# One-core FNet + gated MLP in blocks: loads, differences and copies moved to other places in the queues

## The chip, the cores and the metric

The kernel runs on one core of a Trainium2 chip. The metric is the device time of one execution in microseconds, the median of several. Lower is better. The profile is of one execution of its own. Engines are named as the profile names them: PE is TensorE's matmuls and PEld its weight loads, DVE is VectorE, ACT is ScalarE, POOL is GpSimd, SP is SyncE, which issues most of the DMAs.

## The reference

```python
def _A_ref(x, dft_seq_re, dft_seq_im, dft_hid_re, dft_hid_im):
    a = jnp.einsum("bsd,ed->bse", x, dft_hid_re)
    b = jnp.einsum("bsd,ed->bse", x, dft_hid_im)
    y = jnp.einsum("ts,bse->bte", dft_seq_re, a) - jnp.einsum("ts,bse->bte", dft_seq_im, b)
    return y

def _B_ref(x, W_gate, W_up, W_down):
    gate = jnp.einsum("bsd,df->bsf", x, W_gate)
    up = jnp.einsum("bsd,df->bsf", x, W_up)
    gate = gate * (gate > 0)
    h = gate * up
    return jnp.einsum("bsf,fd->bsd", h, W_down)

xn = _layernorm(x, axis=-1)
return x + _A_ref(xn, ...) + _B_ref(xn, W_gate, W_up, W_down)
```

There are 2048 tokens of width 640, the inner width of the gated part is 1728, and everything is float32.

## The kernel before

**Precision.** Every float32 operand is split into a high part and a low part: ScalarE copies it (line 125), which rounds it to the matmul's format, and VectorE subtracts that copy from the original to get the low part (line 126). A product is then three matmuls: high by high (line 131), high by low (line 132), low by high (line 133). So a block of 128 x 1024 costs one ScalarE and one VectorE instruction before TensorE can use it. TensorE needs the high part for the first of the three matmuls and the low part for the second.

**Three stages.** The first stage normalises the tokens in groups of 256 (`next_group`, groups 0 to 7) and multiplies them by the sequence DFT matrices. The second is the gate and up products. The third, opened at line 1089, multiplies the results of both by the hidden DFT matrices and by the down weights, adds the residual and writes the output. All three use a two-by-two block scheme with seven products in place of eight (Winograd's form), so operands are often sums or differences of blocks.

**The last stage.** `project(q)` runs for two halves of the tokens, called pairs here: first q = 1, then q = 0. Each pair has seven products in the order B11, T1, B21, T2, B22, T3, T4, so B22 is the fifth and T4 the seventh. Each product runs over seven units, numbered 0 to 6: units 0 to 2 come from the DFT half (two with 1024 columns, one with 512), 3 to 5 from the gated half, 6 is the rest (64 rows, `short`, in B21, B22 and T4). T4 runs unit 6 before unit 5. A unit's name such as T2.6 means unit 6 of T2. A unit of 1024 columns has 18 matmuls in the products that have three outputs (B11, T1, B21, B22) and 12 in the others.

For each unit there are three steps. `load` issues its DMAs: the raw block of the moving operand (`get`, tile `rw`, or `re` for unit 6) and its weights. The weights are either raw and split on the chip (tile `wr`, then `wt`), in B11, T1, B21 and B22, or already split in DRAM (`wt<-wparts`, line 1148), in T2, T3 and T4. `prepare` forms the difference of raw blocks where the product's name begins with T (line 1162), then splits the block into tile `cb` and the weights into `wt`. `run` issues the matmuls. `drive(4, 2)` calls `load` four units ahead of `run` and `prepare` two units ahead.

Raw blocks stay in 24 buffers (`raws`), since several products use them. With r11, r12, r21, r22 for the four raw blocks of a unit, the differences are made in place: T1 makes r12 := r12 - r11, T2 makes r12 := r22 - r12, T3 makes r11 := r12 - r11 and T4 makes r21 := r21 - r12.

**What sets the order.** SP's and GpSimd's instructions keep the order in which the program issues them. SP waits in that order: a load whose buffer is not free holds back all loads behind it. There are 4 buffers for `wr`, 5 for `wt` and 3 for `cb` (the ring). VectorE's, ScalarE's and TensorE's instructions are put in order by a scheduler when the kernel is built, and each engine works through its queue in that fixed order. `in_turn` (BACK = 3) keeps the steps of `prepare` from running far ahead.

**The result of a product** is read from PSUM by VectorE (`add_y`, line 1222) and, when complete, stored by GpSimd's DMA. T2 adds to the banks that B11 filled, T3 and T4 to the same banks again, so T4's first matmul follows the read of T3's sums.

**Group 4.** In the first stage half of the groups is one block row of the scheme. Before group 4, the sums of groups 0 to 3 are copied from PSUM by ScalarE (`keep_first`, tile `sa`, line 122), and group 4's matmuls (line 499) go on adding to the same banks. `next_group(4)` forms the normalised tokens: VectorE centres them, ScalarE writes their high part to `xs_late` (line 232), VectorE the low part (line 236). In this kernel ScalarE has the high part of the first half of the tokens, then the three copies, then the high part of the second half.

Of the kernel before, what the change touches and what calls it, by code (L numbers as in the profile page):

```python
# [7 lines left out]
F32 = mybir.dt.float32  # L8
# [4 lines left out]
P = 128  # L13
S, D, F = 2048, 640, 1728
KD = D // P
CH = 512
# [3 lines left out]
SG = 2  # L20
NG = S // (P * SG)
NH = NG // 2
# [5 lines left out]
NF = F // P  # L28
REST = F - NF * P
# [29 lines left out]
def fnet_reglu_kernel(  # L59
# [178 lines left out]

    def keep_a21(g, src=None):

        nc.gpsimd.dma_start(xn_block(g, K2, 0).bitcast(F32), ln_place(g)[:, :, K2] if src is None else src)

    def pin(steps):
        return [tc.keep_in_program_order(i) for i in steps]
# [6 lines left out]
    def next_group(g, b, raw, before):  # L251

        xs, bs, mv = ln_tiles(g)
        js = slice(0, SG)
        cs = K14 if g < NH else slice(0, D)
        low = lambda engine, j: pin([engine.tensor_tensor(flat(b, 1)[:, j], raw[:, j], flat(b, 0)[:, j].bitcast(F32), op=OP.subtract)])
        pin(ln_stats(g, xs, bs, mv, js))
        pin([nc.scalar.activation(flat(b, 0), raw, AF.Copy)])
        if before is not None:
            behind_vector(before)  # L260
            for j in range(SG):
                low(nc.gpsimd, slice(j * CH, (j + 1) * CH))
# [11 lines left out]
        if before is None:  # L274
            for j in range(SG):
                low(nc.vector, slice(j * CH, (j + 1) * CH))
        pin(ln_refine(g, mv, js))
        late["ln"] = pin(ln_low(g, xs, j, cs) for j in range(SG)[: 1 if g == NH else SG])[-1].ins
        if g == NH:

            def second():
                late["high"] = pin([ln_high(g, xs, mv, 1, cs)])[0].ins
                late["ln"] = pin([ln_low(g, xs, 1, cs)])[0].ins

            late["second"] = second
        if g < NH:
            late["a21"] = g, xs, mv
# [263 lines left out]
    def first_stream(c, name, g):  # L551
# [537 lines left out]
    for n, b, side in (("wraw", 4, "left"), ("ring2", 3, "left"), ("wts", 5, "left"), ("raws", 24, "left"), ("ends", 4, "right"), ("y", 1, "right")):  # L1089
        open_pools[n] = ctx.enter_context(tc.tile_pool(name=n, bufs=b, side=side, reuse_waits="tile"))  # L1090

    def project(q):
        c0, c1 = 2 * q, 2 * q + 1
        units = [("hid", u) for u in HID_UNITS] + [("f", u) for u in F_UNITS] + [("end", (NF // 2,))]
        raws, B, y = {}, {}, {}
        a, b2 = slice(0, REST), slice(REST, 2 * REST)

        def get(kind, u):
            what, ks = units[u]
            o = raws[kind, u] = (pool("ends").tile([P, 1, CH], F32, name="re") if what == "end" else  # L1100
                                 pool("raws").tile([P, 2, CH], F32, name="rw")[:, : len(ks)])
            col, row = int(kind in ("B12", "B22")), int(kind in ("B21", "B22"))
            if what == "hid":
                nc.sync.dma_start(o, pqd[(c0, c1)[col]][row][:, ks[0] : ks[-1] + 1])
            elif what == "end" and row:
                if col:
                    nc.gpsimd.memset(o[b2], 0.0)
                nc.sync.dma_start(o[a, 0], hrest[q][:, col * CH : (col + 1) * CH])
            else:
                nc.sync.dma_start(o, hd[q][2 * ks[0] + row : 2 * ks[-1] + row + 1 : 2][:, :, col * CH : (col + 1) * CH].rearrange("f p t -> p f t"))  # L1110

        def unit(name, u, first, last):
            what, ks = units[u]
# [5 lines left out]
            def load():  # L1119
                kind = {"T1": "B12"}.get(name, name)  # L1120
                if name == "B11" and (q, u) == (1, 0):
                    return
                if kind in ("B11", "B12", "B21"):
                    get(kind, u)

                ahead = {("B21", 1): 0, ("B21", 3): 1, ("B21", 5): 2, ("T2", 0): 3, ("T2", 2): 4, ("T2", 3): 5, ("T2", 4): 6}.get((name, u))
                if ahead is not None:
                    get("B22", ahead)
                if name == "B11" and ("B11", 0) not in raws:
                    get("B11", 0)  # L1130
                own, sums = [i.rearrange("k p n -> p k n") for i in pair(k0, n)], wparts[:, k0 : k0 + n]
                if short and name == "T4":
                    w = pool("wts").tile([P, 2, 2, 3 * P], F32R, name="wt").rearrange("p k v n -> p (k v n)")[:, : 4 * P]
                    t["w"] = w.rearrange("p (k v n) -> p k v n", k=1, v=2)
                    nc.sync.dma_start(w.bitcast(F32), wend)
                    return
                if short:
                    t["r"] = r = pool("wraw").tile([P, 2, 3 * P], F32, name="wr")[:, :n]
                    if name == "B21":
                        nc.sync.dma_start(r[a], own[1][:, :, : 3 * P])  # L1140
                    else:
                        nc.sync.dma_start(r[a, :, :P], own[1][:, :, 2 * P : 3 * P])
                        nc.sync.dma_start(r[a, :, P:], sums[a, :, Z4 : Z4 + 2 * P])
                    return
                if name in PARTS:
                    w = pool("wts").tile([P, 2, 2, 3 * P], F32R, name="wt").rearrange("p k v n -> p (k v n)")[:, : n * 4 * P]
                    t["w"] = w.rearrange("p (k v n) -> p k v n", k=n, v=2)
                    nc.sync.dma_start(w.rearrange("p (k n) -> p k n", k=n).bitcast(F32), sums[:, :, HIGH + PARTS[name] :][:, :, : 4 * P])  # L1148
                    return
                t["r"] = r = pool("wraw").tile([P, 2, 3 * P], F32, name="wr")[:, :n]  # L1150
                if name in ("B11", "B21"):
                    nc.sync.dma_start(r, own[name == "B21"][:, :, : 3 * P])
                else:
                    z = (Z1, Z4)[name == "B22"]
                    nc.sync.dma_start(r[:, :, :P], own[name == "B22"][:, :, 2 * P : 3 * P])  # L1155
                    nc.sync.dma_start(r[:, :, P:], sums[:, :, z : z + 2 * P])

            def prepare():
# [1 line left out]
                    t.update(lead)  # L1160
                    return
                sub = lambda o, i0, i1: nc.vector.tensor_tensor(o, i0, i1, op=OP.subtract)
                r = lambda kind: raws[kind, u]
# [142 lines left out]
```

## Time and profile before

| | |
|---|---|
| median of three runs | 1029.99 us (1029.58 to 1030.07) |
| the profiled execution | 1030.06 us |
| its span, first to last instruction | 1028.3 us |
| granted TensorE clock | 0.999 |
| TensorE busy | 1021.8 us of 4520 matmuls |
| VectorE busy | 819.2 us |
| ScalarE busy | 434.2 us |
| moved by DMA | 246.02 MB, mean 239 GB/s |

The first stage ends and the second begins near 400 us; the last stage begins near 731 us with q = 1, and q = 0 begins near 877 us. A row of a timeline holds the start, the duration, the engine, the line, the operation, the tiles written and read, the shape, and how often it came; in brackets stands how long the engine was idle before it and what ended that. A row of the windows view holds a stretch, its length and, for PE, PEld, DVE, ACT and POOL, the busy time and the number of instructions; then the granted clock, the share of the DMA engines' time and GB/s. A row of DMA issues holds the tiles, how many, KB each, and the median time from issue to landing. A matmul's end is modelled, so matmuls are compared by their starts: in steady work they stand 0.23 us apart.

### The profile page before, as it was taken

To read this page: it belongs to the slowest core of one execution; us is meant where nothing else is said; L and a number is where in the kernel's file an instruction comes from. 1 tells how busy PE (TensorE), PEld (TensorE's weight loads), DVE (VectorE), ACT (ScalarE), POOL (GpSimd) and SP (SyncE) were. 2 spreads that over 40 slices of the span, in tenths; PEclk is the share of its full clock that TensorE was granted. 3 is DMA by queue.
4 is the path that set the end of the run, shared out by engine and by line. 5 is a ranking of instruction groups with operands and counts; after the bars stand their busy time and mean duration, and the time that the engine had idled before them with its cause. 6 is when DMAs were issued, how large, how long until landed. Compare 5 with 4: busy or idle time off the path is not lost.

```text
span 1028.3 us, 12571 instructions
## 1 busy us (share of the span) xinstructions
PE 1021.8 (99%) x4520; PEld 843.5 (82%) x4520; DVE 819.2 (80%) x1117; ACT 434.2 (42%) x552; POOL 124.3 (12%) x195
## 2 busy tenths in 40 slices
PE   9999999999999999999999999999999999999998
PEld 8888888888888888888888888888888888888886
DVE  7967987998989586788878988887686778866785
ACT  5554453343433333433335443443454433544532
POOL 3431001022110002411110000011000000000000
PEclk9999999999999999999999999999999999999999
DMA  8887734967969885763474665674895838993654
GB/s 304 313 293 287 264 119 170 335 227 255 353 224 339 312 321 163 250 215 133 148 242 153 219 236 215 225 264 148 305 335 171 274 98 272 384 336 119 211 176 160
DMA packets 95326, 246.02 MB, mean 239 GB/s; under 512 B 11488, under 2 KB 35552, under 8 KB 92576
## 3 DMA queue, kind: packets, MB, share of 16 engines
q1 hardware_dynamic: 77088, 173.12, 49.0%
q0 software_dynamic: 18176, 72.10, 18.9%
q8 instruction: 35, 0.57, 0.2%
q14 instruction: 27, 0.22, 0.1%
HBM read 184.09 MB, written 60.05 MB: 237 GB/s over the span
## 4 chain that ended last, share of the span: by engine, by line
PE 97%; DMA 1%; DVE 0%; SPq 0%; ACT 0%; issue 0%; ACTq 0%
PE ps L132 31%; PE ps L131 31%; PE ps L133 31%; PE ps L499 3%; PE ps L528 1%; DMA wr<-in_hid 1%; PE ps L1206 1%; DMA wr<-wparts 1%; PE ps L113 1%; DVE cb L126 0%; ACT cb L125 0%; SPq L1155 0%; DVE wt L126 0%; ACT wt L125 0%; SPq L1148 0%
## 5 line engine op out<-in xcount | busy, mean ns | idle before, releaser
L132 PE MATMUL ps<-cb,wt 128*128 128x512 f32 x410 | 159.9, 390 | 0.6 <-DVE cb L126 0.6
L131 PE MATMUL ps<-cb,wt 128*128 128x512 f32 x410 | 159.7, 389 | 0.3 <-issue 0.3
L133 PE MATMUL ps<-cb,wt 128*128 128x512 f32 x410 | 159.2, 389 | 0.0
L125 ACT ACTIVATE cb<-rw 128x1024 fp32r<-128x1024 f32 x83 | 82.0, 989 | 122.8 <-PE ps L133 105.9
L126 DVE TENSOR_TENSOR cb<-rw,cb 128x1024 fp32r<-128x1024 f32 x83 | 93.1, 1132 | 43.4 <-ACT cb L125 43.3
L125 ACT ACTIVATE cb<-raw 128x1024 fp32r<-128x1024 f32 x71 | 75.4, 1062 | 113.7 <-PE ps L133 106.2
L126 DVE TENSOR_TENSOR cb<-raw,cb 128x1024 fp32r<-128x1024 f32 x71 | 86.8, 1223 | 39.0 <-ACT cb L125 38.7
L131 PE MATMUL ps<-xs_early,gw 128*128 128x512 f32 x260 | 101.2, 389 | 0.0
L133 PE MATMUL ps<-xs_early,gw 128*128 128x512 f32 x260 | 101.2, 389 | 0.0
L132 PE MATMUL ps<-xs_early,gw 128*128 128x512 f32 x260 | 101.1, 389 | 0.0
L132 PEld LDWEIGHTS ps<-cb,wt 128*128 128x128 f32 x410 | 77.0, 188 | 17.6 <-DVE cb L126 1.9
L131 PEld LDWEIGHTS ps<-cb,wt 128*128 128x128 f32 x410 | 77.0, 188 | 17.1 <-ACT cb L125 1.1
L131 PE MATMUL ps<-cb,xs_late 128*128 128x512 f32 x232 | 90.2, 389 | 0.0
L132 PE MATMUL ps<-cb,xs_late 128*128 128x512 f32 x232 | 90.2, 389 | 0.0
L133 PE MATMUL ps<-cb,xs_late 128*128 128x512 f32 x232 | 90.2, 389 | 0.0
L133 PEld LDWEIGHTS ps<-cb,wt 128*128 128x128 f32 x410 | 77.0, 188 | 15.9
L122 ACT ACTIVATE gw<-z 128x1024 fp32r<-128x1024 f32 (+1 forms) x52 | 57.6, 1110 | 76.5 <-DVE z L834 76.5
L131 PE MATMUL ps<-cb,xs_early 128*128 128x512 f32 x226 | 87.9, 389 | 0.0
L132 PE MATMUL ps<-cb,xs_early 128*128 128x512 f32 x226 | 87.9, 389 | 0.0
L133 PE MATMUL ps<-cb,xs_early 128*128 128x512 f32 x226 | 87.9, 389 | 0.0
L122 ACT ACTIVATE u<-ps 128x512 f32<-128x512 f32 x52 | 31.2, 599 | 90.4 <-PE ps L133 90.4
L844 DVE TENSOR_TENSOR gw<-z,gw 128x1024 fp32r<-128x1024 f32 (+1 forms) x52 | 64.7, 1284 | 3.8 <-ACT gw L122 3.8
(183 smaller groups left out, 1972.7 us busy)
## 6 DMA issues: line engine op xcount, KB each, us to landing
raw<-in_dft SPq DMA_DIRECT2D x94, 512.0 KB, 5.8
z<-in_wgu SPq DMA_DIRECT2D x26, 640.0 KB, 3.9
wt<-wparts SPq DMA_DIRECT2D x30, 512.0 KB, 4.4
hd<-ob POOLq DMA_DIRECT2D x26, 512.0 KB, 3.3
wparts<-pw POOLq DMA_DIRECT2D x12, 1024.0 KB, 4.1
rw<-hd SPq DMA_DIRECT2D x24, 512.0 KB, 5.9
tk<-in_dft SPq DMA_DIRECT2D x16, 512.0 KB, 7.3
set<-r POOLq DMA_DIRECT2D x16, 512.0 KB, 3.7
```

Of the source, the lines that this page charges most:

```text
L113: nc.tensor.matmul(ps[:, :P], warm, warm, start=True, stop=True)
L122: return nc.scalar.activation(o, i, AF.Copy)
L125: nc.scalar.activation(hi, src, AF.Copy)
L126: return nc.vector.tensor_tensor(lo, src, hi.bitcast(F32), op=OP.subtract)
L131: nc.tensor.matmul(ps, wh, mh, start=first, stop=False, skip_group_check=more)
L132: nc.tensor.matmul(ps, wh, ml, start=False, stop=False, skip_group_check=more)
L133: nc.tensor.matmul(ps, wl, mh, start=False, stop=last, skip_group_check=more)
L499: start["pe"] = pin([nc.tensor.matmul(E[0, key], xn_part(n * SG + j, d)[v == 1], b[:, int(v == 2), j], start=False, stop=n % NH == NH - 1 ...
L528: pin([nc.tensor.matmul(E[c, key], xn_part(j, d)[v == 1], b[c][0][:, int(v == 2), j], start=j == 0 and v == 0, stop=False)])
L844: tt(self.w[:, 1, cs], self.z[:, cs], self.w[:, 0, cs].bitcast(F32), op=OP.subtract)
L1206: nc.tensor.matmul(B[out], w[:, 0, v, oo : oo + P], b[:, 0, 0], start=False, stop=last and v == 1, skip_group_check=more)
```

## The change

Four edits.

1. In `next_group`, for group 4 everything from the centring of the tokens on (`finish`) runs after the three copies of `keep_first`; before, only the second half's high and low parts did.
2. B22's raw blocks are issued with T1.3, T1.5, B21.0, B21.1, B21.3, B21.4 and B21.5. Before, they were issued with B21.1, B21.3, B21.5, T2.0, T2.2, T2.3 and T2.4.
3. T4's differences are formed in B22's `prepare`, after the split of the B22 block of the same unit, and T4's `prepare` only splits.
4. The first three raw blocks of B11 of the second pair (q = 0) are issued in T4 of the first pair, with its units 1, 3 and 5. For this `raws` is shared by both pairs.

```diff
@@ next_group
-            keep_a21(late.pop("keep"))
+            pin([keep_a21(late.pop("keep"))])
         root, inverse = ln_first(g, mv, js)
         pin([root])
         pin([ln_mean(g, mv, js)])
-        pin([ln_center(xs, mv, 0, cs)])
-        pin([inverse()])
-        pin([ln_high(g, xs, mv, 0, cs)])
-        pin([ln_center(xs, mv, 1, cs)])
-        if g != NH:
+
+        def finish():
+            pin([ln_center(xs, mv, 0, cs)])
+            pin([inverse()])
+            pin([ln_high(g, xs, mv, 0, cs)])
+            pin([ln_center(xs, mv, 1, cs)])
             late["high"] = pin([ln_high(g, xs, mv, 1, cs)])[0].ins
...
+            pin(ln_refine(g, mv, js))
+            late["ln"] = pin(ln_low(g, xs, j, cs) for j in range(SG))[-1].ins
+            if g < NH:
+                late["a21"] = g, xs, mv
+
         if g == NH:
...
+            late["finish"] = finish
+            return
+        finish()
@@ keep_first
             for i, key in enumerate((("e1", 0), ("e1", 1), "v1")):
                 pin([copy(t["first"][:, i], E[c, key])])
-            late["second"]()
+            late["finish"]()
@@ project, load
-                if kind in ("B11", "B12", "B21"):
-                    get(kind, u)
-
-                ahead = {("B21", 1): 0, ("B21", 3): 1, ("B21", 5): 2, ("T2", 0): 3, ("T2", 2): 4, ("T2", 3): 5, ("T2", 4): 6}.get((name, u))
+                if kind in ("B11", "B12", "B21") and (q, kind, u) not in raws:
+                    get(q, kind, u)
+
+                ahead = {("T1", 3): 0, ("T1", 5): 1, ("B21", 0): 2, ("B21", 1): 3, ("B21", 3): 4, ("B21", 4): 5, ("B21", 5): 6}.get((name, u))
                 if ahead is not None:
-                    get("B22", ahead)
+                    get(q, "B22", ahead)
...
+                if name == "T4" and q == 1 and u in (1, 3, 5):
+                    get(0, "B11", u // 2)
@@ project, prepare
                     elif name == "T4":
 
-                        src, at = r("B21"), a if short else slice(0, P)
-                        sub(src[at], src[at], r("B12")[at])
+                        src = r("B21")
...
+                    if name == "B22":
+                        at = a if short else slice(0, P)
+                        sub(r("B21")[at], r("B21")[at], r("B12")[at])
```

In the built program TensorE's order is the same. On SP, B22's and B11's loads stand where the edits put them. On GpSimd the memset that B22.6 needs goes ahead of the stores of the products. On VectorE and ScalarE the scheduler's order changes around the places named, and in T1 and B21 of the first pair and B11 of the second as well.

More of the change, by code (lines that the diff above doesn't have):

```diff
@@ L267, in next_group @@
         pin([ln_mean(g, mv, js)])
-        pin([ln_center(xs, mv, 0, cs)])
-        pin([inverse()])
-        pin([ln_high(g, xs, mv, 0, cs)])
-        pin([ln_center(xs, mv, 1, cs)])
-        if g != NH:
-            late["high"] = pin([ln_high(g, xs, mv, 1, cs)])[0].ins
[L274 to L278, printed above, removed]
-        if g == NH:
[L281 to L287, printed above, removed]
+        def finish():
[3 more added lines that the diff above has]
+            pin([ln_center(xs, mv, 1, cs)])
+            late["high"] = pin([ln_high(g, xs, mv, 1, cs)])[0].ins
+            if before is None:
+                for j in range(SG):
+                    low(nc.vector, slice(j * CH, (j + 1) * CH))
+            pin(ln_refine(g, mv, js))
+            late["ln"] = pin(ln_low(g, xs, j, cs) for j in range(SG))[-1].ins
+            if g < NH:
+                late["a21"] = g, xs, mv
+        if g == NH:
+            late["finish"] = finish
+            return
+        finish()
         if g == NG - 1:
@@ L1090, in fnet_reglu_kernel, with get @@
         open_pools[n] = ctx.enter_context(tc.tile_pool(name=n, bufs=b, side=side, reuse_waits="tile"))
+    units = [("hid", u) for u in HID_UNITS] + [("f", u) for u in F_UNITS] + [("end", (NF // 2,))]
+    a, b2 = slice(0, REST), slice(REST, 2 * REST)
+    raws = {}
+    def get(q, kind, u):
+        what, ks = units[u]
+        o = raws[q, kind, u] = (pool("ends").tile([P, 1, CH], F32, name="re") if what == "end" else
+                                pool("raws").tile([P, 2, CH], F32, name="rw")[:, : len(ks)])
+        col, row = int(kind in ("B12", "B22")), int(kind in ("B21", "B22"))
+        cs = slice(col * CH, (col + 1) * CH)
+        if what == "hid":
+            nc.sync.dma_start(o, pqd[2 * q + col][row][:, ks[0] : ks[-1] + 1])
+        elif what == "end" and row:
+            if col:
+                nc.gpsimd.memset(o[b2], 0.0)
+            nc.sync.dma_start(o[a, 0], hrest[q][:, cs])
+        else:
+            nc.sync.dma_start(o, hd[q][2 * ks[0] + row : 2 * ks[-1] + row + 1 : 2][:, :, cs].rearrange("f p t -> p f t"))
     def project(q):
         c0, c1 = 2 * q, 2 * q + 1
[L1094 to L1110, printed above, removed]
+        B, y = {}, {}
         def unit(name, u, first, last):
@@ L1122, in load @@
                     return
[L1123 to L1126 removed]
+                if kind in ("B11", "B12", "B21") and (q, kind, u) not in raws:
+                    get(q, kind, u)
+                ahead = {("T1", 3): 0, ("T1", 5): 1, ("B21", 0): 2, ("B21", 1): 3, ("B21", 3): 4, ("B21", 4): 5, ("B21", 5): 6}.get((name, u))
                 if ahead is not None:
[L1128 to L1130 removed]
+                    get(q, "B22", ahead)
+                if name == "B11" and (q, "B11", 0) not in raws:
+                    get(q, "B11", 0)
+                if name == "T4" and q == 1 and u in (1, 3, 5):
+                    get(0, "B11", u // 2)
                 own, sums = [i.rearrange("k p n -> p k n") for i in pair(k0, n)], wparts[:, k0 : k0 + n]
@@ L1162, in prepare @@
                 sub = lambda o, i0, i1: nc.vector.tensor_tensor(o, i0, i1, op=OP.subtract)
-                r = lambda kind: raws[kind, u]
+                r = lambda kind: raws[q, kind, u]
                 with in_turn():
```

2 lines of the change are left out of this document (1 added, 1 removed).

## The prediction

> **What bounds the kernel now.** I read the page's first two parts, then TensorE's own timeline wherever one matmul starts later than the usual 0.23 us after the one before, then what the other engines did there. The page first:
>
> ```profile
> span 1028.3 us, 12571 instructions
> PE 1021.8 (99%) x4520; PEld 843.5 (82%) x4520; DVE 819.2 (80%) x1117; ACT 434.2 (42%) x552; POOL 124.3 (12%) x195
> ```
>
> TensorE is busy 99% of the span, and the diff adds or removes no matmul. The change can only fill or open gaps between matmuls. The gaps in the places it touches are these (chain of waits in the first stage; TensorE's timeline at the heads of B22 of the first pair, T4 of the first pair, B11 of the second pair and B22 of the second pair):
>
> ```profile
> by line: PE ps L499 51.8%; PE ps L132 16.5%; PE ps L133 16.4%; PE ps L131 15.9%
> 31.28 4.08 PE ps L499 x18
> 39.44 4.86 PE ps L499 x18
> ```
>
> ```profile
> 820.25 0.39 PE L131 MATMUL ps<-cb,wt 128*128 128x512 f32 x1
> 820.61 0.50 PE L132 MATMUL ps<-cb,wt 128*128 128x512 f32 x1
> ...
> 859.73 0.39 PE L133 MATMUL ps<-cb,wt 128*128 128x512 f32 x1
> ...
> 860.96 0.47 PE L131 MATMUL ps<-cb,wt 128*128 128x512 f32 x1 [0.16 <-issue]
> ...
> 876.93 0.39 PE L131 MATMUL ps<-cb,wt 128*128 128x512 f32 x1
> 877.68 0.50 PE L132 MATMUL ps<-cb,wt 128*128 128x512 f32 x1 [0.36 <-DVE cb L126]
> 878.02 0.39 PE L133 MATMUL ps<-cb,wt 128*128 128x512 f32 x1
> ...
> 966.67 0.39 PE L131 MATMUL ps<-cb,wt 128*128 128x512 f32 x1
> 967.31 0.50 PE L132 MATMUL ps<-cb,wt 128*128 128x512 f32 x1 [0.25 <-DVE cb L126]
> ```
>
> Start to start, less 0.23: group 4 loses 4.86 - 4.08 = 0.78 us, B22 of the first pair 0.13, T4 0.32 (860.96 - 859.73, four starts), the change of pair 0.52, B22 of the second pair 0.41. After such a wait the third matmul is late too (878.02 - 877.68 - 0.23 = 0.11), so four of these places hold 0.11 more each. All that could be won is near 2.6 us, and 0.2% of the run, about what a measurement of this kernel tells from no change, is 2.06 us.
>
> **Group 4's copies first.** ScalarE's timeline there:
>
> ```profile
> 37.85 0.83 ACT L232 ACTIVATE xs_late<-r,mv 128x640 fp32r<-128x640 f32 x1 [1.74 <-DVE mv L211]
> 38.70 1.57 ACT L122 ACTIVATE sa<-ps 128x512 f32<-128x512 f32 x3
> ```
>
> The three copies (1.57 us) empty the sums that group 4's first matmuls add to, and stand behind a scaling that waited 1.74 us for VectorE. What they read was finished at 31.28 + 4.08 = 35.4, so in the new order they go into that idle time, from 36.1 to 37.7, and the scaling still starts at 37.85 and ends at 38.7, before the matmul at 39.4. Gain 0.78; lower bound 0, should another operand be late. In the built order GpSimd's store of a kept block (L241) also goes behind two subtractions, and two first-stage loads change places in SP's queue. The by-line row has only TensorE in this window, so TensorE waits for neither: 0.
>
> **B22's seven blocks earlier, both pairs.** Per pair seven issues on SP move: two go from B21 into T1, one moves up within B21, four go from T2 into B21. The last one needs a memset on GpSimd first. That memset moves ahead of the result stores in GpSimd's queue; it needs nothing but its tile, and GpSimd is busy 12% of the run, so it delays no store. In T1 the traffic is heavy, but what ScalarE waits for there is TensorE freeing the ring, not a load. The stage's row (its last two numbers are the DMA engines' busy share and GB/s) and one such wait:
>
> ```profile
> 755.60:780.10 24.50, 24.50 (x109) 20.29 (x109) 18.82 (x23) 11.83 (x15) 0.00 (x0) 1.00 0.94 334
> ```
>
> ```profile
> 759.98 1.06 ACT L125 ACTIVATE cb<-rw 128x1024 fp32r<-128x1024 f32 x1 [2.71 <-PE ps L133]
> ```
>
> Two blocks more in T1 are 1.05 MB, 3.1 us at 334 GB/s, met block by block by waits like the 2.71; I take 0 (bound 0.4 us a pair if one block comes 3.1 late against 2.71).
>
> What B22 waited for is not these blocks but its weights. VectorE at the head of B22, first pair, then second pair:
>
> ```profile
> 814.37 0.69 DVE L126 TENSOR_TENSOR cb<-re,cb 128x512 fp32r<-128x512 f32 x1 [1.06 <-ACT cb L125]
> 817.43 1.91 DVE L126 TENSOR_TENSOR wt<-wr,wt 128x768 fp32r<-128x768 f32 x2 [2.37 <-ACT wt L125]
> 819.33 1.23 DVE L126 TENSOR_TENSOR cb<-rw,cb 128x1024 fp32r<-128x1024 f32 x1
> ...
> 964.06 1.98 DVE L126 TENSOR_TENSOR wt<-wr,wt 128x768 fp32r<-128x768 f32 x2 [2.58 <-ACT wt L125]
> ```
>
> ```profile
> 963.18 0.85 ACT L125 ACTIVATE wt<-wr 128x768 fp32r<-128x768 f32 x1 [2.43 <-DMA wr<-wparts]
> ```
>
> Weights of units 0 and 1, then the block of unit 0, which TensorE wants for its second matmul. The weights' landing starts it.
>
> **T4's differences in B22.** This is where it costs. The built order on VectorE was: T2.6's low part, weights 0, weights 1, block 0. It becomes: difference 0, weights 0, T2.6's low part, difference 1, weights 1, block 0; ScalarE likewise puts T2.6 behind weights 0. Difference 0 fits into the idle time before the landing. T2.6's part (it used to run at 814.37, in idle time) and difference 1 now stand after it, ahead of block 0. Their prices, start to start, from rows of the same shapes, with the read of T3's sums that the T4 wait needs:
>
> ```profile
> 859.04 1.22 DVE L1162 TENSOR_TENSOR rw<-rw 128x1024 f32<-128x1024 f32 x1
> 860.18 0.68 DVE L1222 TENSOR_TENSOR y<-ps,y 128x512 f32<-128x512 f32 x1
> ```
>
> A full difference is 860.18 - 859.04 = 1.14, its 1.22 less 0.08 of overlap; T2.6's half-width part is 0.69 less the same, 0.61, taken as 0.60: together 1.74 us more between the landing and block 0. T2.6 itself is safe: its low part would be done at 817.43 - 0.43 + 0.95 + 0.69 = 818.6 with the landing taken below, and its second matmul, five before 820.25, is at 819.1.
>
> Against that, the weights land earlier by what left the queue ahead of them. Of the moved loads only the last (128 KB, on 64 partitions) was still under way:
>
> ```profile
> 804.15 0.46 SPq L1108 DMA_DIRECT2D re<-hr  x1
> 804.78 5.12 SPq L1148 DMA_DIRECT2D wt<-wparts  x3
> ```
>
> ```profile
> DMA packets 3440, 4.61 MB, mean 308 GB/s; under 512 B 281, under 2 KB 2032, under 8 KB 3440
> ```
>
> At the 308 GB/s of 803 to 818 us it is 0.43 us. From below 0, if the three result stores and weight blocks in that window fill the room; from above 0.43 plus the 0.63 by which SP issues the next block sooner (804.78 - 804.15), 1.06. I take 0.43, since issues that wait for TensorE follow. The Trainium skill has another price: its page "SBUF — State Buffer", section "Door 1: The DMA port swizzle", gives a transfer on partitions 0 to 63 half the ports and 196 GB/s measured; as an estimate that is 0.67 us, and the sum below would be 1031.2. No row here times that load alone.
>
> So B22 loses 1.74 - 0.43 = 1.31 in the first pair, and in the second 1.25 (its two weights take 1.98 instead of 1.91, a wait of some 0.06 that goes): 2.56 together, between 1.3 (1.06 twice) and 3.4 (0). Behind block 0 stand a half difference, weights 2, the read of T2's sums and block 1, some 3 us of work (three of the smaller kind at 0.60 or less, one at 1.14), which TensorE wants after 18 more matmuls (4.1 us). So the lag ends there; the stage had
>
> ```profile
> 820.20:844.30 24.10, 24.10 (x106) 19.64 (x106) 17.75 (x21) 10.19 (x13) 0.00 (x0) 1.00 0.30 87
> ```
>
> 6.3 us idle for the five later differences (3 x 1.14 + 2 x 0.60 = 4.6). If that cover were gone, each full difference would cost its 1.14.
>
> T4 does not win what its lighter queue suggests. Its 0.32 us is the wait for T3's sums to be read out of the bank. The last rows of the run show how soon a read can follow the bank's last matmul:
>
> ```profile
> 1022.04 0.39 PE L133 MATMUL ps<-cb,wt 128*128 128x512 f32 x1
> ...
> 1022.47 0.69 DVE L1222 TENSOR_TENSOR y<-ps,y 128x512 f32<-128x512 f32 x1 [2.62 <-PE ps L133]
> ```
>
> 0.43 us. T3's first bank gets its last matmul at 859.73 (the three after it are the second bank's); the read could start at 860.16 and did at 860.18. Gain 0.02 a pair.
>
> **The second pair's first blocks ahead.** The change of pair:
>
> ```profile
> 866.70 0.37 SPq L1148 DMA_DIRECT2D wt<-wparts  x1
> 867.12 0.58 SPq L1104 DMA_DIRECT2D rw<-pq  x1
> 867.75 0.43 SPq L1152 DMA_DIRECT2D wr<-in_hid  x1
> ```
>
> ```profile
> 874.57 0.85 ACT L125 ACTIVATE wt<-wr 128x768 fp32r<-128x768 f32 x1 [2.68 <-DMA wr<-in_hid]
> 875.33 1.99 ACT L125 ACTIVATE cb<-rw 128x1024 fp32r<-128x1024 f32 x2
> ```
>
> ```profile
> 860.90:877.00 16.10, 16.04 (x71) 13.25 (x71) 10.97 (x12) 6.87 (x8) 1.08 (x2) 1.00 0.94 328
> ```
>
> Again the weights were last. A 512 KB block leaves the queue ahead of them, a 256 KB one enters: 256 KB at 328 GB/s, 0.80 us sooner, or 1.43 with the issue moved up by 0.63. But both built queues now put weights 1 ahead of block 0: 0.76 (875.33 - 874.57) more, or 1.2 if ScalarE has to wait for its 393 KB at 328 GB/s. Net from 0.67 sooner to 0.4 later. I take 0, near the middle.
>
> The entered block also goes ahead of T4's own last weights. These were issued at 866.70 and took 5.6 us:
>
> ```profile
> wt<-wparts SPq DMA_DIRECT2D x1, 512.0 KB, 5.6
> ```
>
> landing at 872.3, and their 12 matmuls, the last before 876.93, begin at 876.93 - 12 x 0.23 = 874.2. 1.9 us of cover against 0.80: nothing.
>
> **The sum.** -0.78 - 0.04 + 0 + 2.56 = +1.74. The profiled execution took 1030.06 (its span 1028.3 and 1.8 around it), 0.07 over the median, so 1031.8 for it and 1031.7 for the median: 0.17% more, within 0.2%.
>
> **The rivals.** *The landing does not move.* If stores and weight blocks fill the room, both B22 heads pay the whole 1.74 and 1.68: 1029.99 - 0.82 + 3.42 = 1032.6, slower. For it: the DMA engines are busy throughout that window. Against: 128 KB really are gone. It decides from a landing less than 0.27 us sooner.
>
> *The weights land unhindered.* How long 256 KB take, at B22's head and in a quiet stretch (838 to 844 us):
>
> ```profile
> wr<-wparts SPq DMA_DIRECT2D x1, 256.0 KB, 6.0
> ```
>
> ```profile
> wt<-wparts SPq DMA_DIRECT2D x1, 256.0 KB, 2.5
> ```
>
> If taking loads out brought 6.0 near 2.5, 3.5 us cover the 1.74: B22's gaps (0.13, 0.41) close, and the pair's 0.52, with the 0.11 behind each of the three. 1029.99 - 0.82 - 1.06 - 0.33 = 1027.8, faster. Against it: one load of ten has left. "SBUF — State Buffer" of the Trainium skill, section "The DMA setup-cost knee", has 2 us plus bytes at 436 GB/s, an estimate of 2.6 for 256 KB; the trace agrees in the quiet stretch alone.
>
> *Only group 4 counts*: the weights land about 1.7 us sooner, gaps stay as they are. 1029.99 - 0.82 = 1029.2, no change.
>
> **How the numbers follow.** Forecast 0.52, with its own range 1030.5 to 1032.0; landing unmoved (or another late operand) 0.33; only group 4, or the way to it, 0.10; unhindered 0.05. So slower 0.33, within 0.2% 0.62, faster 0.05. The range 1029.2 to 1033.0 reaches from the case of group 4 alone to the unmoved landing with the 0.4 of the change of pair on top; it leaves out the unhindered case and part of the tails.
>
> **What would show it.** Group 4's 18 matmuls back at 4.08; at B22's heads gaps of 1.2 to 1.9 us with the block's low part as what ended them, VectorE running T2.6 and a difference between the two weights; T4's first gap still 0.3; the change of pair anywhere from 0 to 0.9. The forecast is wrong if B22's heads show no gap over 0.5, or if a gap opens in T1 or B21.

## The result

| | before | after |
|---|---|---|
| median of 18 runs | 1030.14 us | 1031.80 us |
| ratio of the changed kernel to before, 95% interval | | 1.0016 [1.0009, 1.0024] |
| span of the profiled execution | 1028.3 us | 1030.4 us |

The change makes the kernel 1.7 us slower, 0.16%, where 1.7 us had been forecast. The first two lines of the page after:

```profile
span 1030.4 us, 12571 instructions
PE 1021.4 (99%) x4520; PEld 843.9 (82%) x4520; DVE 817.8 (79%) x1117; ACT 433.8 (42%) x552; POOL 125.0 (12%) x195
```

TensorE's work is the same, so the 2.1 us between the two spans are gaps between matmuls. Group 4 first, in the chain of waits of the changed kernel (start, length, what; its line 498 is line 499 of the kernel before), and then ScalarE's timeline there:

```profile
39.52 4.08 PE ps L498 x18
```

```profile
36.26 1.58 ACT L122 ACTIVATE sa<-ps 128x512 f32<-128x512 f32 x3
37.71 1.56 ACT L232 ACTIVATE xs_late<-r,mv 128x640 fp32r<-128x640 f32 x2
```

The 18 matmuls are back at 4.08 us from 4.86, because the copies run before the scaling. TensorE's timeline of the changed kernel at the same four places as before, B22 of the first pair, T4, the change of pair and B22 of the second pair:

```profile
819.56 0.39 PE L131 MATMUL ps<-cb,wt 128*128 128x512 f32 x1
821.30 0.50 PE L132 MATMUL ps<-cb,wt 128*128 128x512 f32 x1 [1.35 <-DVE cb L126]
...
861.10 0.39 PE L133 MATMUL ps<-cb,wt 128*128 128x512 f32 x1
861.64 0.47 PE L131 MATMUL ps<-cb,wt 128*128 128x512 f32 x1 [0.15 <-issue]
...
877.66 0.49 PE L131 MATMUL ps<-cb,wt 128*128 128x512 f32 x1
878.92 0.50 PE L132 MATMUL ps<-cb,wt 128*128 128x512 f32 x1 [0.76 <-DVE cb L126]
...
967.95 0.39 PE L131 MATMUL ps<-cb,wt 128*128 128x512 f32 x1
969.47 0.50 PE L132 MATMUL ps<-cb,wt 128*128 128x512 f32 x1 [1.13 <-DVE cb L126]
```

Start to start less 0.23, the gaps are 1.51 (821.30 - 819.56 - 0.23), 0.31, 1.03 and 1.29 us. Before they were 0.13, 0.32, 0.52 and 0.41. Three of the four are ended by the low part of block 0. VectorE's timeline of the changed kernel at B22 of the first pair, at B11 of the second pair and at B22 of the second pair shows what stands ahead of it:

```profile
812.53 1.22 DVE L1166 TENSOR_TENSOR rw<-rw 128x1024 f32<-128x1024 f32 x1
816.55 0.96 DVE L126 TENSOR_TENSOR wt<-wr,wt 128x768 fp32r<-128x768 f32 x1 [2.80 <-ACT wt L125]
817.42 0.68 DVE L126 TENSOR_TENSOR cb<-re,cb 128x512 fp32r<-128x512 f32 x1
818.03 1.22 DVE L1166 TENSOR_TENSOR rw<-rw 128x1024 f32<-128x1024 f32 x1
819.16 0.95 DVE L126 TENSOR_TENSOR wt<-wr,wt 128x768 fp32r<-128x768 f32 x1
820.03 1.22 DVE L126 TENSOR_TENSOR cb<-rw,cb 128x1024 fp32r<-128x1024 f32 x1
...
875.73 1.92 DVE L126 TENSOR_TENSOR wt<-wr,wt 128x768 fp32r<-128x768 f32 x2 [1.93 <-DMA wr<-in_hid]
877.64 2.36 DVE L126 TENSOR_TENSOR cb<-rw,cb 128x1024 fp32r<-128x1024 f32 x2
...
968.20 1.22 DVE L126 TENSOR_TENSOR cb<-rw,cb 128x1024 fp32r<-128x1024 f32 x1
```

L1166 is the difference. At B22 difference 0 is done before the weights land; then come weights 0, T2.6's block, difference 1, weights 1 and only then block 0, at 820.03, when TensorE already wants it. At the change of pair both weights stand ahead of block 0. The landing itself is read from ScalarE, which splits the weights as soon as they are there. First pair, change of pair, second pair:

```profile
815.67 0.85 ACT L125 ACTIVATE wt<-wr 128x768 fp32r<-128x768 f32 x1 [4.31 <-DMA wr<-wparts]
...
874.85 1.81 ACT L125 ACTIVATE wt<-wr 128x768 fp32r<-128x768 f32 x2 [2.30 <-DMA wr<-in_hid]
...
963.83 0.85 ACT L125 ACTIVATE wt<-wr 128x768 fp32r<-128x768 f32 x1 [4.09 <-DMA wr<-wparts]
```

Two numbers describe each head, the first matmuls of a product. The *lead* is the time from ScalarE's start on weights 0 to the start of block 0's first matmul, less any delay of that matmul itself: 819.56 - 815.67 = 3.89 us, against 820.25 - 816.55 = 3.70 before. The *way* is the time from ScalarE's start on weights 0 to VectorE's start on block 0: 820.03 - 815.67 = 4.36, against 2.78 before. The gap grows by what the way grows, less what the lead grows.

| | lead before, after | way before, after | gap by that | gap in the trace |
|---|---|---|---|---|
| B22, first pair | 3.70, 3.89 | 2.78, 4.36 | +1.39 | 0.13 to 1.51 |
| B22, second pair | 3.49, 4.12 | 2.85, 4.37 | +0.89 | 0.41 to 1.29 |
| change of pair | 2.36, 2.78 | 1.83, 2.79 | +0.54 | 0.52 to 1.06 (with 0.03 ahead of the first matmul) |

With group 4's -0.78 and T4's -0.01 a pair, the sum is +2.0 of the 2.1 us between the spans.

### The profile page after: what moved, and what is told of

Its sections match the earlier page's. It is cut to its first block, busy times and chain, and to the rows that moved or that the text cites. A ratio compares the mean times of both kernels' runs of the same rounds, so it can differ in the third digit from the quotient of the medians.

```text
span 1030.4 us, 12571 instructions
## 1 busy us (share of the span) xinstructions
PE 1021.4 (99%) x4520; PEld 843.9 (82%) x4520; DVE 817.8 (79%) x1117; ACT 433.8 (42%) x552; POOL 125.0 (12%) x195
## 4 chain that ended last, share of the span: by engine, by line
PE 95%; DMA 3%; DVE 1%; ACT 0%; issue 0%; SPq 0%; ACTq 0%
PE ps L132 30%; PE ps L133 30%; PE ps L131 30%; PE ps L498 3%; DMA wt<-wparts 1%; PE ps L527 1%; PE ps L1212 1%; DMA wr<-in_wd 1%; DMA wr<-in_hid 1%; DMA wr<-wparts 1%; PE ps L113 1%; DVE cb L126 0%; ACT cb L125 0%; ACT wt L125 0%; SPq L1152 0%
## 5 line engine op out<-in xcount | busy, mean ns | idle before, releaser
L131 PE MATMUL ps<-cb,wt 128*128 128x512 f32 x410 | 159.8, 390 | 0.3 <-issue 0.3
L133 PE MATMUL ps<-cb,wt 128*128 128x512 f32 x410 | 159.3, 389 | 0.0
L131 PE MATMUL ps<-xs_early,gw 128*128 128x512 f32 x260 | 101.2, 389 | 0.0
L133 PE MATMUL ps<-xs_early,gw 128*128 128x512 f32 x260 | 101.1, 389 | 0.0
L131 PEld LDWEIGHTS ps<-cb,wt 128*128 128x128 f32 x410 | 76.9, 188 | 17.3 <-ACT cb L125 1.4
L131 PE MATMUL ps<-cb,xs_late 128*128 128x512 f32 x232 | 90.2, 389 | 0.0
L133 PE MATMUL ps<-cb,xs_late 128*128 128x512 f32 x232 | 90.2, 389 | 0.0
L133 PEld LDWEIGHTS ps<-cb,wt 128*128 128x128 f32 x410 | 77.0, 188 | 16.0
L131 PE MATMUL ps<-cb,xs_early 128*128 128x512 f32 x226 | 87.9, 389 | 0.0
L133 PE MATMUL ps<-cb,xs_early 128*128 128x512 f32 x226 | 87.9, 389 | 0.0
```

Of the source, the lines that this page charges most:

```text
L131: nc.tensor.matmul(ps, wh, mh, start=first, stop=False, skip_group_check=more)
L133: nc.tensor.matmul(ps, wl, mh, start=False, stop=last, skip_group_check=more)
```

## The experiments

The theory is the prediction's: the order on VectorE and ScalarE between the landing of the weights and block 0 sets the gaps (A). Against it stand the moved transfers themselves (B) and the amount of VectorE work (C). Line numbers of these kernels are a few higher than those of the diff where code was put in: matmuls L133 to L135 in place of L131 to L133, differences L1169, reads of sums L1235 to L1238.

**The order held, nothing else changed.** In B22, and in B11 of the second pair, a unit's weights are split after the block of the unit before, on both engines, and a difference is formed after its own unit's block:

```diff
                     if name == "B22":
                         at = a if short else slice(0, P)
-                        sub(r("B21")[at], r("B21")[at], r("B12")[at])
+                        with tc.issue_after(lows[-1].ins):
+                            sub(r("B21")[at], r("B21")[at], r("B12")[at])
...
-                        split(w[:, :, 0], w[:, :, 1], t["r"])
+                        with ExitStack() as block:
+                            if name == "B22" or (name, q) == ("B11", 0) and u:
+                                block.enter_context(tc.issue_after(lows[-2].ins))
+                                block.enter_context(tc.issue_after(high_of[lows[-2].ins.name].ins))
+                            split(w[:, :, 0], w[:, :, 1], t["r"])
```

> The changed kernel with one thing altered: the order of VectorE's and ScalarE's queues is held so that, in B22 and in B11 of the second pair, a unit's weights are split only after the block of the unit before, and a difference for T4 is formed only after the block of its own unit. Loads and work are the same. Theory A (what stands on VectorE and ScalarE between the landing of B22.0's weights and block 0 sets the gap): the gaps of 1.52, 1.30 and 1.03 us at B22 of the first pair, B22 of the second pair and the change of pair fall to below 0.1, with the 0.11 behind each and the 0.03 ahead of the last: 4.2 us less than the changed kernel's 1031.8, 1027.6 us, faster than before. Theory B (the moved transfers make the weights or blocks land late): the gaps stay above 1 us, 1031.8. Theory C (seven more differences are more VectorE work than B22 has room for): B22's gaps stay above 1 us or go to its later units, above 1031.

Measured: 1028.45 us, ratio to before 0.9984 [0.9975, 0.9992]. VectorE's and then TensorE's timeline of this kernel at the head of B22 of the first pair:

```profile
813.61 0.69 DVE L126 TENSOR_TENSOR cb<-re,cb 128x512 fp32r<-128x512 f32 x1 [1.07 <-ACT cb L125]
816.12 0.96 DVE L126 TENSOR_TENSOR wt<-wr,wt 128x768 fp32r<-128x768 f32 x1 [1.82 <-ACT wt L125]
817.07 1.23 DVE L126 TENSOR_TENSOR cb<-rw,cb 128x1024 fp32r<-128x1024 f32 x1
818.21 1.22 DVE L1169 TENSOR_TENSOR rw<-rw 128x1024 f32<-128x1024 f32 x1
819.35 0.95 DVE L126 TENSOR_TENSOR wt<-wr,wt 128x768 fp32r<-128x768 f32 x1
```

```profile
819.49 0.39 PE L133 MATMUL ps<-cb,wt 128*128 128x512 f32 x1
819.72 0.39 PE L134 MATMUL ps<-cb,wt 128*128 128x512 f32 x1
```

Block 0 now follows weights 0 at once and is done at 818.30 for a matmul at 819.72. The second matmul follows the first after 0.23 us at all three heads. The same loads, the same differences and the same amount of work cost nothing when they stand behind block 0. B and C fall. The median is 3.4 us below the changed kernel's, of 4.2 expected. In the profiled executions TensorE's last matmul starts at 1021.18 us here and at 1025.57 in the changed kernel, 4.4 us sooner. The spans differ by 3.9 (1030.4 to 1026.5), so some 0.4 us is lost again behind the last matmul. The changed kernel's profiled execution, 1032.19 us, was also 0.4 above its own median.

**Without the differences.** The third edit taken out of the change.

```diff
-                        src = r("B21")
+                        src, at = r("B21"), a if short else slice(0, P)
+                        sub(src[at], src[at], r("B12")[at])
...
-                    if name == "B22":
-                        at = a if short else slice(0, P)
-                        sub(r("B21")[at], r("B21")[at], r("B12")[at])
```

> The changed kernel with the differences of T4 formed in T4 again, everything else of the change kept. VectorE's order at the head of B22 is then weights 0, T2.6's low part, weights 1, block 0. Theory A: each head loses one full difference of 1.14 us, so 1.52 and 1.30 become 0.38 and 0.16; 2.3 us less, 1029.5 us; the change of pair keeps 1.0 to 1.2. Theory B: the heads keep 1.3 to 1.5, 1031.8. Theory C: the heads fall to the 0.13 and 0.41 of before, 1029.3, so this run tells A from B and leaves A and C together.

Measured: 1029.82 us, 0.9997 [0.9986, 1.0008]. B22's gaps are 0.0 in both pairs, smaller than expected, since the leads were 4.27 and 4.46 in this execution against 3.89 and 4.12. The way is 3.23 in both pairs, 1.13 less than the 4.36, one difference. The change of pair lost 1.94 us and then more (last section).

**The differences alone.** The third edit put into the kernel before (the diff above the other way round, on that kernel).

> The kernel before with the third edit alone: T4's differences formed in B22. The built order puts differences 0 and 1 ahead of weights 0, T2.6 between them. Theory A: both stand ahead of the landing, in 1.06 + 2.37 us of idle time on VectorE, and block 0 stands where it did: B22's gaps 0.13 and 0.41 as before, T4's 0.30, 1030.1 us. Theory C: the same 14 differences cost what they cost in the changed kernel, about 1.1 us a pair: 1032.4. Theory B says nothing of it (no load is moved): 1030.1.

Measured: 1030.74 us, 1.0010 [1.0001, 1.0019]. VectorE's timeline at the head of B22:

```profile
818.88 0.68 DVE L126 TENSOR_TENSOR cb<-re,cb 128x512 fp32r<-128x512 f32 x1
819.48 1.21 DVE L1162 TENSOR_TENSOR rw<-rw 128x1024 f32<-128x1024 f32 x1
821.73 1.89 DVE L126 TENSOR_TENSOR wt<-wr,wt 128x768 fp32r<-128x768 f32 x2 [1.03 <-ACT wt L125]
823.60 1.22 DVE L126 TENSOR_TENSOR cb<-rw,cb 128x1024 fp32r<-128x1024 f32 x1
```

Difference 1 (L1162), like difference 0 ahead of it, runs before the weights' 821.73, and 1.03 us of idle time is left. The gaps are 0.15 and 0.09 us. The same 14 differences that add 1.13 us to the way in the changed kernel add nothing here. C's 1032.4 is not met. The 0.6 us over before is at the edge of its interval. The profiled execution, 1034.32 us, had a stall of 2.6 us near 451 us, in the second stage, which the edit doesn't touch, and lost some 1.7 us more behind it at a granted clock of 0.55 (last section). Matched matmul by matmul with the kernel before, it lost nothing in the last stage: it stood 4.3 us behind at the stage's start and 3.8 at the last matmul. Whether part of the 0.6 between the medians belongs to the edit stays open.

**The loads alone.** The second edit put into the kernel before: only the table of the places.

```diff
-                ahead = {("B21", 1): 0, ("B21", 3): 1, ("B21", 5): 2, ("T2", 0): 3, ("T2", 2): 4, ("T2", 3): 5, ("T2", 4): 6}.get((name, u))
+                ahead = {("T1", 3): 0, ("T1", 5): 1, ("B21", 0): 2, ("B21", 1): 3, ("B21", 3): 4, ("B21", 4): 5, ("B21", 5): 6}.get((name, u))
```

> The kernel before with the second edit alone: B22's seven blocks issued earlier. The built order puts T2.6's low part behind weights 0. Theory A: 0.60 us more between landing and block 0 in each pair, less the sooner landing (0.19 and 0.63 us in the profile of the changed kernel): gaps of 0.5 and 0.4 in place of 0.13 and 0.41, 1030.1 to 1030.6 us. Theory B (the moved transfers cost the time by themselves): gaps of over 1 us, 1032. If the landing were not sooner at all: gaps of 0.73 and 1.01, 1031.3.

Measured: 1030.43 us, 1.0004 [0.9991, 1.0017]. VectorE's timeline at the head of B22 of the first pair:

```profile
817.37 0.96 DVE L126 TENSOR_TENSOR wt<-wr,wt 128x768 fp32r<-128x768 f32 x1 [3.83 <-ACT wt L125]
818.24 0.68 DVE L126 TENSOR_TENSOR cb<-re,cb 128x512 fp32r<-128x512 f32 x1
818.84 0.95 DVE L126 TENSOR_TENSOR wt<-wr,wt 128x768 fp32r<-128x768 f32 x1
819.71 1.22 DVE L126 TENSOR_TENSOR cb<-rw,cb 128x1024 fp32r<-128x1024 f32 x1
```

T2.6's block stands behind weights 0 here too, with no difference moved. So that part of the way comes with the second edit. From weights 0 to block 0 it is 2.34 us against 1.90 before: 0.44 us. The gaps are 0.27 and 0.0, as the leads of 4.00 and 4.40 have it.

**Group 4 alone.** The first edit put into the kernel before.

> The kernel before with the first edit alone: group 4's copies ahead of everything from the centring on. By the prediction's own step: group 4's 18 matmuls go from 4.86 us back to 4.08 start to start, 0.7 to 0.8 us less, 1029.4 us; every gap of the last stage as before (0.1 to 0.5 at B22's heads, 0.3 at T4, 0.4 to 0.9 at the change of pair). Rival: another operand of group 4 is late, or the displaced scaling opens a gap elsewhere in the first stage: 1030.1.

Measured: 1029.62 us, 0.9998 [0.9989, 1.0006]. No gap is left at group 4 (18 matmuls 0.23 apart), and the last stage has those of the kernel before (0.37 and 0.25 at B22, 0.75 at the change of pair). The 0.78 are there in the trace and within the noise of the time.

**T3's last two units exchanged**, on top of the held order. The edit also makes T4's second unit wait for VectorE's reads of T3's sums (`seen["y"]`), and puts two empty steps behind T4's first unit, so that its second is prepared after those reads:

```diff
-            if name == "T4":
+            if name in ("T3", "T4"):
                 us[-2:] = us[:-3:-1]
...
                 with in_turn(), ExitStack() as sums_read:
+                    if (name, u) == ("T4", 1):
+                        sums_read.enter_context(tc.issue_after(seen["y"].ins))
...
+                if (name, u) == ("T4", 0):
+                    todo.extend([(idle, idle, idle, idle)] * 2)
```

> The kernel of e1_block_first with T3's last two units exchanged, so that the last unit gives each bank six matmuls in place of three and the first bank is finished 1.36 us before T3 ends in place of 0.68; VectorE reads both of T3's sums before it splits T4's second block. Theory A (T4's first gap is the read of the bank: the read starts 0.43 us after the bank's last matmul and takes 0.69): the read ends before T4 wants the bank, the gap of 0.31 with 0.08 behind it closes in both pairs, 0.8 us less than e1_block_first, 1027.7. Rival (the gap is T4's first block or its weights): it stays, 1028.4.

Measured: 1027.44 us, 0.9978 [0.9968, 0.9988]. TensorE's and VectorE's timeline around the end of T3 of the first pair:

```profile
859.37 0.39 PE L135 MATMUL ps<-cb,wt 128*128 128x512 f32 x1
859.60 0.39 PE L133 MATMUL ps<-cb,wt 128*128 128x512 f32 x1
```

```profile
858.44 0.69 DVE L1238 TENSOR_TENSOR y<-ps,y 128x512 f32<-128x512 f32 x1 [0.40 <-PE ps L135]
859.80 0.69 DVE L1238 TENSOR_TENSOR y<-ps,y 128x512 f32<-128x512 f32 x1 [0.67 <-PE ps L135]
```

The read of the first bank is over at 859.13 and T4's first matmul, at 859.60, follows its predecessor by 0.23. So the gap that the change could not close was the read of the bank, as the prediction had it. This version is faster than both kernels: 2.6 us less than before.

**Group 4 and the held order, without the moved loads and differences.** The first edit and the order of the first experiment in the kernel before.

> The kernel before with the first edit and with the held order of e1_block_first, but no load moved and no difference moved. Theory A: block 0 goes ahead of weights 1 (0.95 us) at B22's heads, so 0.13 and 0.41 close with the 0.11 behind each; with group 4's 0.7 that is 1.4 to 1.5 us less than before, 1028.6; the change of pair keeps its 0.4 to 0.9. If the moved loads and differences of the change are worth something once the order is right, this stays more than 1 us behind e1_block_first, above 1029.4.

Measured: 1029.22 us, 0.9989 [0.9980, 0.9998]. Both B22 gaps are closed, as expected. The change of pair lost 1.3 us in the profiled execution, at a lead of 1.68, more than the 0.8 us by which this kernel stands behind the first experiment.

**The held order without the second pair's early blocks.** The fourth edit taken out of the first experiment's kernel.

> The kernel of e1_block_first without the fourth edit: the second pair's first blocks are loaded with B11 again. Theory A (these blocks leave the queue ahead of B11.0's weights, which land 0.5 to 0.8 us sooner): the weights land 2.0 to 2.5 us before they are wanted in place of 3.2, and the change of pair opens a gap of 0.4 to 0.9 again with 0.11 behind it: 0.5 to 1.0 us more than e1_block_first, 1029.0 to 1029.4. If the landing does not depend on these blocks: no gap, 1028.4.

Measured: 1029.07 us, 0.9992 [0.9984, 1.0001]. TensorE's timeline at the change of pair:

```profile
875.94 0.39 PE L133 MATMUL ps<-cb,wt 128*128 128x512 f32 x1
876.72 0.50 PE L134 MATMUL ps<-cb,wt 128*128 128x512 f32 x1 [0.39 <-DVE cb L126]
```

The gap is back, 0.55 us, at a lead of 2.33. By the medians the early blocks are worth 0.6 us once the order is right, which the gap and the 0.11 behind it agree with.

**The held order without the differences.** The first experiment's kernel with the differences in T4.

> The kernel of e1_block_first with T4's differences formed in T4 again. Theory A: once block 0 stands ahead of them, the differences cost nothing in B22 and bring nothing in T4 but the 0.01 us a pair of its first gap: 1028.4 us, as e1_block_first. If e3_differences_alone's 0.6 us over the kernel before belongs to the differences: 0.6 less than e1_block_first, 1027.8. If T4 was short of VectorE time: gaps in T4, above 1028.8.

Measured: 1028.09 us, 0.9979 [0.9971, 0.9988], between the two values expected. VectorE's last read starts at 1021.58 us here and at 1021.61 in the first experiment's profile, while the spans are 1026.0 and 1026.5: up to the last matmul the two are alike, and the half microsecond lies behind the last sum, where the two kernels have the same two stores. What sets it stays open.

**The order held at the change of pair alone**, B22 as in the change.

> The changed kernel with the order held at B11 of the second pair alone: weights 1 behind block 0, as in the kernel before; B22's heads as the change has them. Theory A: one weight split of 0.95 us leaves the way from the landing to block 0, so the change of pair's gap falls from 1.03 to below 0.1 with the 0.11 behind it, and B22's heads keep gaps of 0.9 to 1.5: 1.0 to 1.1 less than the changed kernel, 1030.7. If the gap there is the landing alone: 1.0 stays, 1031.8.

Measured: 1031.41 us, 1.0014 [1.0005, 1.0023]. The gap at the change of pair is 0.0 (0.08 behind it), B22's are 1.31 and 1.52: the place is as A has it. The time is 0.7 above the number expected.

**The last of the seven blocks late again.** One entry of the table on the first experiment's kernel:

```diff
-("B21", 5): 6}
+("T2", 4): 6}
```

> The kernel of e1_block_first with the last of B22's seven blocks (128 KB on 64 partitions) issued with T2's fifth unit again, the other six as in the change. With all seven moved B22.0's weights landed 3.98 to 4.57 us ahead of the need, with none moved 3.58 to 3.90. The prediction's step (only the last load was still under way): 3.6 to 3.9 in both pairs. Rival (the whole load of the queue counts): near 4.2, between the two. The time is e1_block_first's, 1028.4, since the held order leaves over 1 us of room.

Measured: 1028.38 us in one run. The weights landed 3.64 and 4.15 us ahead of the need (ScalarE starts on them 0.1 us later, so these are leads of 3.56 and 4.07), one value in the range of each theory. This does not settle whether the last block alone or the queue's whole load brings the landing forward.

**T3's units exchanged, without the differences.** The sixth experiment's kernel with the differences in T4.

> The kernel of e6_t3_units_swapped with T4's differences formed in T4 again. VectorE's order around the end of T3 then has the difference of T4's fourth unit ahead of the read of the first bank and that of its second unit between the read of the second bank and the block. Theory A (a VectorE instruction costs only where it stands between the last arrival and what TensorE wants next): here two differences of 1.14 us do stand there. The first read starts 0.4 us later and T4's first gap is 0.1 to 0.3; the second block's low part ends 6.1 us after T3's last unit began, where TensorE wants it at 5.7, a gap of 0.2 to 0.5: 0.3 to 0.5 us a pair more than e6_t3_units_swapped's 1027.4, 1028.0 to 1028.4. Rival (where the differences are formed no longer matters once B22's order is held, as e9_order_without_differences had it): no gap in T4, 1027.4.

Measured: 1029.89 us, 1.0001 [0.9992, 1.0010]. VectorE's timeline in T4:

```profile
859.02 1.35 DVE L1235 TENSOR_TENSOR y<-ps,y 128x512 f32<-128x512 f32 x2
860.28 1.22 DVE L1169 TENSOR_TENSOR rw<-rw 128x1024 f32<-128x1024 f32 x1
862.71 1.83 DVE L126 TENSOR_TENSOR cb<-rw,cb 128x1024 fp32r<-128x1024 f32 x2 [1.21 <-ACT cb L125]
```

2.4 us more than with the differences in B22, where 0.6 to 1.0 had been expected. The place was right, the size was not: the expectation left out that ScalarE copies the block only after its difference, so VectorE idles 1.21 us between the two. Here the third edit is worth 2.4 us.

## Why the prediction was right

**The sum.** +1.66 us between the medians against a forecast of +1.7. At B22's two heads, where nearly all of the forecast came from, it is the predicted mechanism. That the number came out so close is partly luck. Two misses of opposite sign offset each other: the change of pair lost 0.54 us where 0 had been forecast, and B22's heads lost 2.26 us in place of 2.56. And between the profiled executions, from which the terms are read, the change cost 2.1 us (1032.19 - 1030.06), not 1.7.

- **Group 4**: 0.78 forecast, 4.86 to 4.08 in the trace.
- **The way at B22**: 1.74 and 1.68 us more forecast, 1.58 and 1.52 measured. The difference cost its 1.14, as the row had it. T2.6's block cost 0.44 in place of 0.60. In the run with the loads alone VectorE's weights follow each other and what comes next after 0.87 us (817.37 to 818.24); before, two took 1.90 up to block 0, since VectorE waited for ScalarE, as the row below shows. T2.6's block went into those 0.16 us.
- **Whose cost it is**: the prediction put T2.6's move under the differences. The run with the loads alone has the same order, so it belongs to the second edit.
- **The landing at B22**: 0.43 us sooner forecast. Leads over all profiles: 4.20 us on the mean of the 18 heads with all loads moved (nine kernels, 3.86 to 4.55), 3.66 on the mean of the eight with none moved (four kernels, 3.48 to 3.79): 0.54 sooner. In the changed kernel's own profile it was 0.19 and 0.63, which is why the first pair lost 1.38 and the second 0.88, for 1.31 and 1.25 forecast; in the first pair the way and the landing both came out short, by 0.16 and 0.24, and nearly cancel. That the last of the seven loads alone brings the landing forward, as the prediction had it, is not shown: the run with that block late again leaves it open.
- **The change of pair**, the term that was off most: 0 forecast, +0.54 measured. "I take 0, near the middle" weighed 0.80 sooner against 0.76 to 1.2 of order. The order cost 0.96. The landing came 0.42 sooner in that profile; the mean lead of the seven kernels with the early blocks and B11 right behind an undisturbed T4 is 2.84 us, against 2.16 of the six without them, 0.68 sooner. The landing had been sized from the mean rate of its queue, 0.80 us, and the order taken near the bottom of its range of 0.76 to 1.2. The gap of 1.03 us also lies outside the 0 to 0.9 that the prediction named as a sign of being right.
- **T4**: 0.02 forecast, 0.01 measured, and the bank's read was the cause.
- **No gap in T1 or B21, and none in B22's later units**: TensorE's timeline has none there.
- **The rivals**: the landing did move, by 0.54 us on the mean of the kernels, against the first, though the 0.19 us of the first pair in the changed kernel's profile is under the 0.27 us at which the prediction drew the line; it did not move by the 3.5 us of unhindered weights; and the way was paid, against the third.

ScalarE's split of block 0 in the kernel before, from its timeline; it ends at 819.30, and VectorE started block 0 at 819.33:

```profile
818.26 1.04 ACT L125 ACTIVATE cb<-rw 128x1024 fp32r<-128x1024 f32 x1
```

## What to carry to other kernels

At a change of stage, find the operand that lands last and list what each in-order queue runs between that landing and the first result wanted from it. Here, work in front of the landing filled idle time for nothing, and work between the landing and that result was paid, less the idle time that was left there (0.16 us at T2.6's block). The same instruction of 1.14 us cost 0 or 1.13 by its place. When an edit makes work or data ready earlier, look at where the scheduler then puts it, and hold the order at the heads by hand: that turned 1.7 us lost into 1.7 won.

## What the runs showed of the hardware

TensorE's granted clock fell after 1.5 us of idle time. In the run without the differences the change of pair had two idle times of 0.75 and 0.76 us with one matmul between them. TensorE's timeline of that kernel, and its windows (stretch, length, busy time and number of instructions of PE, PEld, DVE, ACT and POOL, granted clock, DMA share, GB/s):

```profile
877.03 0.50 PE L131 MATMUL ps<-cb,wt 128*128 128x512 f32 x1 [0.75 <-ACT cb L125]
878.29 0.60 PE L132 MATMUL ps<-cb,wt 128*128 128x512 f32 x1 [0.76 <-DVE cb L126]
878.69 0.63 PE L133 MATMUL ps<-cb,wt 128*128 128x512 f32 x1
879.11 0.63 PE L131 MATMUL ps<-cb,wt 128*128 128x512 f32 x1
```

```profile
876.00:878.40 2.40, 0.89 (x4) 0.29 (x3) 2.35 (x4) 2.40 (x5) 0.00 (x0) 1.00 0.70 221
878.40:882.00 3.60, 3.60 (x9) 2.83 (x10) 3.60 (x6) 2.04 (x3) 0.54 (x1) 0.53 1.04 385
882.00:886.00 4.00, 4.00 (x19) 3.29 (x19) 2.22 (x3) 1.79 (x2) 1.09 (x2) 1.00 0.80 248
```

For 3.6 us the granted clock is 0.53, and nine matmuls run in that stretch, 0.43 us apart (879.11 - 878.69 = 0.42) where sixteen would have run 0.23 apart: some 1.6 us lost on top of the wait itself. In the changed kernel one idle time of 1.35 us, ended at 821.30 at B22, left the clock at full speed (windows):

```profile
821.30:825.00 3.70, 3.69 (x16) 3.09 (x17) 3.70 (x6) 0.78 (x2) 0.00 (x0) 1.00 0.41 129
```

In the run with the differences alone, one idle time of 2.46 us, ended at 453.95 us, was followed by the same fall (windows):

```profile
454.00:457.60 3.60, 3.60 (x9) 2.78 (x10) 0.00 (x0) 0.39 (x1) 0.76 (x1) 0.55 0.82 337
```

The Trainium skill, page "TensorE: Matmul & The Clock Gate", section "HAM oscillation — how this bites in real kernels", has the rule that idle gaps of TensorE should stay under about 3.4 us. The trace does not agree with that as a safe bound: 1.5 us of idle time in two pieces within 2.0 us was enough once, 2.46 us in one piece was enough once, and 1.35 us in one piece was not. What decides between 1.35 and 1.5 us, no run here shows.
